# Masks and divisions of two chunks moved to TensorE, and a third chunk's attention started earlier

## The chip, the cores and the metric

The kernel runs on one core of one Trainium2 chip. The metric is the device time of one execution in microseconds; lower is better. The engines are PE (TensorE matmuls; PEld is its weight loads), DVE (VectorE), ACT (ScalarE), POOL (GpSimd) and SP (SyncE, whose queue issues all loads and stores here).

## The reference

Attention with 4 batches, 8 heads, 768 positions and 64 elements per head, and behind it a gated feed-forward layer over its 3,072 tokens. Cut to what matters:

```python
k_sum = k.reshape(B, H, 24, 32, D).max(axis=3)       # a key per block of 32
v_sum = v.reshape(B, H, 24, 32, D).mean(axis=3)
scores_l = scale * q @ k.T, masked to |i - j| < 16    # scale = 1/8
scores_s = scale * q @ k_sum.T + log(32)
a = softmax(concat([scores_l, scores_s]))             # sum + 1e-9 in the division
x = (a @ concat([v, v_sum])) as (3072, 512)
out = ((x @ w_a) * (x @ w_b)) @ w_out                 # d_ff = 1536
```

## The kernel before

**Tokens.** The 3,072 tokens are 12 chunks of 256 (`u` = 0 to 11, three per batch), a chunk is two groups of 128. A group's attention needs the window's 96 keys (and 24 block keys) of each of two halves. Its scores for four pairs of heads fill two PSUM banks of 128x512.

**A group's attention** in chunks 0 and 1: PE transposes the queries (`turn`, L401), ACT copies them (`qT`), PE makes the scores (L600), DVE scales them and adds the mask on the way to SBUF (L619) and takes the maxima (L627), ACT makes eight exponentials with their sums (L636), DVE the reciprocals (L643, L649), POOL divides the 128x512 halves (L653), PE transposes them (L401), ACT copies (L669), PE multiplies by the values (L698), and ACT and DVE split the result into a high and a low part, `x` (L706, L709). Chunks from 2 on use no PE for transposes: DVE does them in 32x256 steps, twelve per group (L685 for the probabilities, L863 for the queries). Chunk 0 has two sets of buffers for its two groups, chunk 1 one set (`s`, `pt`, `vw`, `qT`, banks `o2` and `o3`).

**Weights.** `w_a`, `w_b` and `w_out` come in as 36 parts of 512 KB; `convert(j)`, j = 0 to 17, splits two parts at a time into high and low halves: ACT writes the shifted high bits to SBUF and to bank `c0` (L294), DVE makes three passes per half (L309, L327 into `c1`, L333), ACT casts the high half (L369), POOL makes the low half in two passes (L374, L380). The parts stand in the order a0, b0, out0, a1, and so on.

**Feed-forward.** `item(n, u, f)` is one of 12 slices `f` of `d_ff` of chunk `u`: 24 matmuls up (L906), ACT copy, DVE product (L926), ACT cast (L928), DVE remainder (L931), and 6 matmuls down (L942) into `o0`/`o1` (chunk 1: `o2`/`o3`). An up needs the chunk's `x` and the a and b parts of its slice, a down the out part. `x` has two buffers (`u % 2`). The items of chunks 0 and 1 alternate, chunk 0 ahead by LAG = 4 slices; from chunk 2 on the items stand chunk by chunk.

**Order.** Every step is handed to `Work` with an engine, a rank, an estimate of its length and the names of what it reads and writes. `emit` is a list scheduler: it picks, by rank and by estimated readiness, which step stands next on which engine. So the order on each engine is fixed when the program is built, and an engine waits in order at run time. Ranks (L229): CHAIN 0, FIRST 1 (chunk 0), CONVERT 2 + j/4, NEXT 3 (chunk 1), SOON 5 (chunk 2), PREP 5.5, LATER 6. The attention of chunk 2 and of chunk 3 is handed in behind item (1, 11), and its scores use banks `c0` and `c1`, which the conversions use too. Its second group's probabilities lie in `S1`, a conversion buffer; `qin`, its queries' buffer, serves the last conversions as slot "Q".

Of the kernel before, what the change touches and what calls it, by code (L numbers as in the profile page):

```python
# [15 lines left out]
ALU = mybir.AluOpType  # L16
# [68 lines left out]
def attention_moe(  # L85
# [27 lines left out]
    SIGNS = 2  # L113
    FILL = 2
# [114 lines left out]
    CHAIN, FIRST, CONVERT, NEXT, SOON, PREP, LATER = 0, 1, 2, 3, 5, 5.5, 6  # L229
# [38 lines left out]
    spaces["Q"] = qin.rearrange("p c x -> p (c x)")  # L268
    slots = [("S0", 0), ("S0", 2), ("S1", 2), ("Q", 0), ("S0", 0), ("S0", 2), ("S1", 2), ("S0", 0)]

    def convert(j):
# [3 lines left out]
        if j < NW - 4:  # L275
            space = {12: "W16", 13: "W17"}.get(j, ("W17", "W16", "W15", "S0")[j % 4])
            places = [(space, 0, 2), (space, 1, 3)]
            single = j < 2
        else:
            places = [slots[2 * (j - NW + 4) + h] for h in range(2)]  # L280
            places = [(n, x, x + 1) for n, x in places]
            single = True
# [161 lines left out]
    def first_keys():  # L444
        n = P // BLK
        for i in range(S // P):
# [6 lines left out]
            bk = f"o{i % 4}"  # L453
# [134 lines left out]
    def scores(u, t, qT, qk, s, sk, banks, lead=None):  # L588
        kind = 0 if t == 0 else 2 if t == S // P - 1 else 1
        rank = rank_of(u)  # L590
        m, mk = nml[t % 2], f"nml{t % 2}"

        def fn():
            for c in range(NP):
                for h in range(2):
                    hs = slice(h * D, (h + 1) * D)
                    for e in range(2):
# [5 lines left out]
                            start=True, stop=True, tile_position=(h * D, e * QT),  # L603
                        )

        if lead is None:
            pe(-1, 1.2, [qk] + KT, banks, fn)
        else:
# [22 lines left out]
        for h in range(2):
            l = m[:, 1, h, :]
            for c in range(NP):
                act(
                    rank, 0.385, [f"{mk}m{h}", sk[h]], [f"{mk}l{h}{c}"],
                    lambda h=h, c=c: nc.scalar.activation(  # L636
                        s[h][:, c, :], s[h][:, c, :], AF.Exp, bias=m[:, 0, h, c : c + 1],
                        scale=1.0, accum_out=m[:, 1, h, c : c + 1],
                    ),
                )  # L640
            dve(
                rank, 0.1, (), [f"{mk}l{h}{c}" for c in range(NP)],
                lambda l=l: nc.vector.tensor_scalar(  # L643
                    out=l, in0=l, scalar1=1e-9, scalar2=None, op0=ALU.add
# [3 lines left out]
                rank, 0.1, (), [f"{mk}l{h}{c}" for c in range(NP)],  # L648
                lambda l=l: nc.vector.reciprocal(out=l, in_=l),  # L649
            )  # L650
            pool(
                rank, 1.05, [f"{mk}l{h}{c}" for c in range(NP)], [sk[h]],
                lambda h=h, l=l: nc.gpsimd.tensor_tensor(  # L653
                    out=s[h], in0=s[h], in1=l[:, :, None].broadcast_to([P, NP, P]),
                    op=ALU.mult,
                ),
            )

    def transposes(u, t, s, sk, banks):
# [360 lines left out]
```

## Time and profile before

| | |
|---|---|
| time, median of 3 runs | 712.74 us (712.11 to 713.24) |
| time of the profiled execution | 712.94 us |
| its span on the chip | 711.2 us |
| PE busy | 680.2 us (96% of the span) |
| DVE, ACT, POOL busy | 438.8, 271.9, 190.1 us |
| matmuls up (L906), down (L942) | 420.7 us; 158.0 + 90.7 us |

The span is what the trace covers; 1.7 us of the time lie outside of it. "busy" is the time an engine's instructions took, "idle before" what the engine waited before a group, with the instruction that released it. A line number is one of the listing above.

### The profile page before, as it was taken

How to read it: one execution, taken by the hardware profiler on the slowest of the kernel's cores; microseconds unless marked ns; L12 is line 12 of the kernel's file. 1: busy time of each engine (PE TensorE's matmuls, PEld its weight loads, DVE VectorE, ACT ScalarE, POOL GpSimd, SP SyncE). 2: the span in 40 equal slices, each digit the busy share in tenths (PEclk: the TensorE clock that was granted, in tenths of full speed). 3: DMA queues.
4: the chain of work that ended last, by engine and by line, in shares of the span. 5: the costliest groups of instructions: out<-in, count | busy, mean ns of one | idle time of the engine just before them, and what ended most of it. 6: DMA issues, size and time to landing. Idle time of an engine off the chain costs nothing.

```text
span 711.2 us, 15046 instructions
## 1 busy us (share of the span) xinstructions
PE 680.2 (96%) x5952; PEld 625.5 (88%) x5952; DVE 438.8 (62%) x992; ACT 271.9 (38%) x815; POOL 190.1 (27%) x228
## 2 busy tenths in 40 slices
PE   6676799999999999999999999999999999999997
PEld 5475699998989999999999999999999999999996
DVE  3989898598727677766765776673673662321221
ACT  3878886442333332333332423432332331211211
POOL 5589899412334244113010101110110110000000
PEclk9979999999999999999999999999999999999999
DMA  9996353347214334522210330310310100000000
GB/s 230 283 332 201 127 150 126 63 87 162 54 53 117 80 76 94 95 46 60 71 35 2 82 68 1 86 24 1 83 24 1 53 22 1 31 1 1 30 1 29
DMA packets 154942, 54.83 MB, mean 77 GB/s; under 512 B 132456, under 2 KB 147816, under 8 KB 154872
## 3 DMA queue, kind: packets, MB, share of 16 engines
q1 hardware_dynamic: 154872, 53.88, 31.1%
q8 instruction: 46, 0.75, 0.4%
q14 instruction: 24, 0.20, 0.1%
HBM read 47.12 MB, written 6.29 MB: 75 GB/s over the span
## 4 chain that ended last, share of the span: by engine, by line
PE 82%; DVE 6%; SPq 4%; DMA 3%; ACT 2%; POOL 2%; issue 1%; DVEq 0%; POOLq 0%; ACTq 0%
PE h L906 50%; PE o L942 25%; SPq L225 2%; SPq L254 2%; PE o L698 2%; PE o L600 2%; PE c L600 2%; PE c L698 1%; POOL S L540 1%; DVE pt L685 1%; DMA raw<-in_moe_w_a_dram 1%; DMA S<-in_v_dram 1%; DVE ksum L470 1%; DMA space<-in_k_dram 0%; ACT s L636 0%
## 5 line engine op out<-in xcount | busy, mean ns | idle before, releaser
L906 PEld LDWEIGHTS h<-x,w 128*128 128x128 f32 x3456 | 418.0, 190 | 15.2 <-DVE x L709 2.7
L906 PE MATMUL h<-x,w 128*128 128x256 f32 x3456 | 420.7, 279 | 4.1 <-DVE x L709 2.6
L926 DVE TENSOR_TENSOR h<-h,g 128x256 f32<-128x256 f32 x144 | 62.1, 431 | 173.0 <-ACT g L923 171.6
L942 PE MATMUL o<-w,gh 128*128 128x512 f32 x576 | 158.0, 397 | 4.9 <-ACT gh L928 4.9
L923 ACT COPY g<-h 128x256 f32<-128x256 f32 x144 | 53.7, 373 | 283.7 <-PE h L906 283.0
L942 PEld LDWEIGHTS o<-w,gh 128*128 128x128 f32 x576 | 98.9, 188 | 23.1 <-ACT gh L928 6.6
L653 POOL TENSOR_TENSOR s<-s,nml 128x512 f32<-128x512 f32 x44 | 45.8, 1042 | 257.7 <-DVE nml L649 253.9
L685 DVE STREAM_TRANSPOSE pt<-s 32x256 f32<-32x256 f32 x228 | 99.4, 436 | 8.8 <-POOL s L653 3.9
L942 PE MATMUL o<-w,gl 128*128 128x512 f32 x288 | 90.7, 397 | 0.0
L636 ACT ACTIVATE s<-s,nml 128x128 f32<-128x128 f32 x176 | 68.6, 393 | 50.5 <-DVE nml L627 50.3
L931 DVE TENSOR_TENSOR gl<-h,gh 128x256 fp32r<-128x256 f32 x144 | 60.5, 420 | 30.4 <-ACT gh L928 29.3
L928 ACT CAST gh<-h 128x256 fp32r<-128x256 f32 x144 | 53.5, 372 | 63.7 <-DVE h L926 61.7
L942 PEld LDWEIGHTS o<-w,gl 128*128 128x128 f32 x288 | 53.8, 189 | 11.9 <-issue 0.5
L540 POOL TENSOR_TENSOR S<-S 96x512 f32<-96x512 f32 (+3 forms) x48 | 33.6, 699 | 55.2 <-DMA S<-in_v_dram 44.9
L636 ACT ACTIVATION_READ_ACCUMULATOR s<-s,nml 128x1 f32 x176 | 33.3, 189 | 0.0
L643 DVE TENSOR_SCALAR nml<-nml 128x4 f32<-128x4 f32 x48 | 11.9, 249 | 29.6 <-ACT s L636 29.4
L627 DVE TENSOR_REDUCE nml<-s 128x4 f32<-128x512 f32 x44 | 27.8, 667 | 0.0
L374 POOL TENSOR_TENSOR space<-space,w 128x1024 f32<-128x1024 f32 (+1 forms) x13 | 26.8, 2062 | 3.5 <-ACT w L369 2.7
L380 POOL TENSOR_TENSOR w<-space 128x1024 fp32r<-128x1024 f32 (+1 forms) x13 | 26.7, 2054 | 0.9
L294 ACT ACTIVATE S<-raw 128x1024 f16<-128x1024 f32 (+1 forms) x20 | 23.0, 1149 | 4.8 <-DVE space L309 1.8
L294 ACT ACTIVATE c<-raw 128x512 f32<-128x512 f32 x36 | 23.2, 644 | 1.9 <-DVE space L309 1.2
L436 POOL COPY kT<-ksum 128x144 f32<-128x144 f32 x16 | 4.8, 309 | 57.9 <-DVE ksum L518 44.5
(99 smaller groups left out, 460.4 us busy)
## 6 DMA issues: line engine op xcount, KB each, us to landing
raw<-in_moe_w_a_dram SPq DMA_DIRECT2D x12, 512.0 KB
raw<-in_moe_w_b_dram SPq DMA_DIRECT2D x12, 512.0 KB
raw<-in_moe_w_out_dram SPq DMA_DIRECT2D x12, 512.0 KB
out_dram<-S SPq DMA_DIRECT2D x24, 256.0 KB
qin<-in_q_dram SPq DMA_DIRECT2D x160, 32.0 KB
S<-in_v_dram SPq DMA_DIRECT2D x24, 192.0 KB
vw<-in_v_dram SPq DMA_DIRECT2D x19, 192.0 KB
vw<-in_v_dram SPq DMA_DIRECT2D x19, 128.0 KB
```

Source lines behind the costliest of these rows:

```text
L294: nc.scalar.mul(out=zhalf[:, lo:hi] if out is None else out, in_=high.bitcast(F32), mul=2.0**-112)
L540: lambda: nc.gpsimd.tensor_tensor(out=out, in0=i0, in1=i1, op=ALU.add),
L600: nc.tensor.matmul(bank[banks[h]][es, c * P : (c + 1) * P], qT[hs, c, es], kT[hs, c, c0 : c0 + P], start=True, stop=True, tile_position=(h ...
L636: lambda h=h, c=c: nc.scalar.activation(s[h][:, c, :], s[h][:, c, :], AF.Exp, bias=m[:, 0, h, c : c + 1], scale=1.0, accum_out=m[:, 1, h, ...
L653: lambda h=h, l=l: nc.gpsimd.tensor_tensor(out=s[h], in0=s[h], in1=l[:, :, None].broadcast_to([P, NP, P]), op=ALU.mult,),
L685: lambda js=js, qs=qs: nc.vector.transpose(out=pv[js, :, qs], in_=sv[qs, :, js]),
L906: nc.tensor.matmul(ps, w[:, c, part, :], x[xpart][:, c, :], start=(i == 0), stop=(i == n - 1))
L923: act(CHAIN, 0.38, [hk], [gk], lambda: nc.scalar.copy(out=g, in_=pa))
L926: lambda: nc.vector.tensor_tensor(out=pa, in0=pb, in1=g, op=ALU.mult),
L928: act(CHAIN, 0.41, [hk], [ghk], lambda: nc.scalar.copy(out=gh, in_=pa))
L931: lambda: nc.vector.tensor_tensor(out=gl, in0=pa, in1=gh.bitcast(F32), op=ALU.subtract),
L942: nc.tensor.matmul(bank[ok[j]], (gh if first else gl)[:, js], w[:, :, part, :], start=(f == 0 and first and part == 0), stop=(f == NF - 1 ...
```

## The change

- **Masks.** For chunks 0 and 1, PE writes the mask into the score banks as a product of mask and identity (L598 of the changed kernel), and the scores accumulate on it (L610). The factor 1/8 goes into the copy of the queries (L833). DVE takes the maxima straight from PSUM (L643), the exponentials read PSUM and leave their sums there (L655). L619's eight DVE instructions for these groups are gone.
- **Divisions.** DVE multiplies the identity by the reciprocals (L677), and the PE product of probabilities and that diagonal (L698) divides and transposes at once. The eight POOL multiplies and the eight plain transposes are gone.
- **Two sets** of `s`, `pt`, `vw`, `qT` and of banks (`o0`/`o1`, `o2`/`o3`) serve groups 2 and 3 (chunk 1) as well; `begin` and `end` in `first_attention` hand all four groups in. NEXT goes from 3 to 2.3, LAG from 4 to 2. The key transposes use `c0`, `c1`, `o2`, `o3`.
- **Third chunk.** `attention` becomes a generator; chunk 2's is advanced behind conversion 7 (query loads), 9 (first group to its transposes), 17 (second group's scores) and behind item (0, 11) (the rest). `qin` is no conversion slot any more, and chunk 2's second group uses `s` instead of `S1`.
- Chunks from 2 on keep their masks on DVE, divisions on POOL (now L685), transposes on DVE (now L725).

The diff, cut to its core:

```diff
+    AHEAD = (7, 9, 17)
...
-    CHAIN, FIRST, CONVERT, NEXT, SOON, PREP, LATER = 0, 1, 2, 3, 5, 5.5, 6
+    CHAIN, FIRST, CONVERT, NEXT, SOON, PREP, LATER = 0, 1, 2, 2.3, 5, 5.5, 6
...
-    spaces["Q"] = qin.rearrange("p c x -> p (c x)")
-    slots = [("S0", 0), ("S0", 2), ("S1", 2), ("Q", 0), ("S0", 0), ("S0", 2), ("S1", 2), ("S0", 0)]
+    slots = [("S0", 0), ("S0", 2), ("S1", 2)]
...
-            bk = f"o{i % 4}"
+            bk = ("c0", "c1", "o2", "o3")[i % 4]
...
+        masked = u < FILL
+
+        def masks():
+            for h in range(2):
+                nc.tensor.matmul(
+                    bank[banks[h]].rearrange("p (c x) -> p c x", x=P), ident,
+                    mask[:, kind, None, :].broadcast_to([P, NP, P]), start=True, stop=False,
+                )
 
...
-                            start=True, stop=True, tile_position=(h * D, e * QT),
+                            start=not masked, stop=not masked or c == NP - 1,
+                            tile_position=(h * D, e * QT),
...
+        if masked:
+            pe(rank + 0.1, 1.8, [], banks, masks)
...
+        x = [bank[n].rearrange("p (c x) -> p c x", x=P) for n in banks] if masked else s
+        xk = banks if masked else sk
...
+            sums = x[h][:, :, 0] if masked else l
...
+            if masked:
+                d, dk = diag
+                dve(
+                    rank, 0.6, lk + [xk[h]], dk[h],
+                    lambda h=h, r=r, d=d: nc.vector.tensor_tensor(
+                        out=d[:, h], in0=ident[:, None, :].broadcast_to([P, NP, P]),
+                        in1=r[:, :, None].broadcast_to([P, NP, P]), op=ALU.mult,
+                    ),
+                )
+            else:
+                pool(
+                    rank, 1.05, lk, [sk[h]],
+                    lambda h=h, r=r: nc.gpsimd.tensor_tensor(
+                        out=s[h], in0=s[h], in1=r[:, :, None].broadcast_to([P, NP, P]),
+                        op=ALU.mult,
+                    ),
+                )
...
+            def turned(h):
+                for c in range(NP):
+                    nc.tensor.matmul(
+                        bank[banks[h]][:, c * P : (c + 1) * P], s[h][:, c, :], d[:, h, c, :],
+                        start=True, stop=True,
+                    )
...
+        pts = [PD, (x.rearrange("p (h c x) -> p h c x", h=2, x=P), [[key[0]], [key[1]]])]
+        def begin(g, bk):
+            u, i = g // G, g % G
+            x, key = queries[g]
+            rank = rank_of(u) + 0.2 * i
+            pe(rank, 0.85, [key], [bk], lambda: turn(bank[bk], x))
             act(
-                FIRST, 0.6, [f"h{t}"], [qTk[t]],
-                lambda t=t: nc.scalar.copy(
-                    out=qT[t], in_=bank[f"h{t}"].rearrange("p (c x) -> p c x", x=P)
+                rank, 0.6, [bk], [qTk[i]],
+                lambda: nc.scalar.mul(
+                    out=qT[i], in_=bank[bk].rearrange("p (c x) -> p c x", x=P), mul=0.125
                 ),
             )
+            scores(u, g, qT[i], qTk[i], s[i], sk[i], [f"o{2 * i}", f"o{2 * i + 1}"], pts[i])
+
+        def end(g, bk):
+            u, i = g // G, g % G
+            transposes(u, g, s[i], sk[i], [f"o{2 * i}", f"o{2 * i + 1}"], pts[i])
...
+        end(0, "h1")
+        load_values(0, 2, vbuf, VK[:3], 20.5)
+        begin(2, "o0")
+        end(1, "h0")
+        load_values(0, 3, vw1, vk1[:3], 20.7)
+        begin(3, "o2")
+        end(2, "o0")
+        end(3, "o2")
...
         if u == FILL:
+            yield
+            begin(0)
+            turned(0)
+            yield
+            begin(1)
+            yield
+            values(*end(0))
+            bring(1)
+            turned(1)
+            values(*end(1))
+        elif u == FILL + 1:
...
-    LAG = 4
+    LAG = 2
...
+    third = attention(FILL)
...
+        if j in AHEAD:
+            next(third)
         item(n, u, f)
-        if (u, f) == (1, NF - 1):
-            attention(2)
-            attention(3)
-        elif f == NF - 1 and 1 < u < NU - 2:
-            attention(u + 2)
+        if (u, f) == (0, NF - 1):
+            next(third)
+        elif f == NF - 1 and u < NU - 2:
```

**PE at the start of the program.** `space8`/`space9` hold keys, `o0` to `o3`, `c0`, `c1`, `h0`, `h1` are PSUM banks. Before:

```order
L401 MATMUL o0_71<-ident_66,space8_188 128x128 x4
L401 MATMUL o1_72<-ident_66,space8_188 128x128 x4
L401 MATMUL o2_73<-ident_66,space8_188 128x128 x4
L401 MATMUL o3_74<-ident_66,space8_188 128x128 x4
L401 MATMUL o0_71<-ident_66,space9_189 128x128 x4
L401 MATMUL o1_72<-ident_66,space9_189 128x128 x4
L401 MATMUL h0_75<-ident_66,space9_189 128x128 x4
L401 MATMUL h1_76<-ident_66,space9_189 128x128 x4
L600 MATMUL o0_71<-kT_79,qT_183 64x128 x2
L600 MATMUL o1_72<-kT_79,qT_183 64x128 x2
```

After:

```order
L598 MATMUL o0_71<-mask_86,ident_66 128x512
L598 MATMUL o1_72<-mask_86,ident_66 128x512
L401 MATMUL c0_77<-ident_66,space8_188 128x128 x4
L401 MATMUL c1_78<-ident_66,space8_188 128x128 x4
L401 MATMUL o2_73<-ident_66,space8_188 128x128 x4
L401 MATMUL o3_74<-ident_66,space8_188 128x128 x4
L401 MATMUL c0_77<-ident_66,space9_189 128x128 x4
L401 MATMUL c1_78<-ident_66,space9_189 128x128 x4
L598 MATMUL o2_73<-mask_86,ident_66 128x512
L598 MATMUL o3_74<-mask_86,ident_66 128x512
L401 MATMUL h0_75<-ident_66,space9_189 128x128 x4
L401 MATMUL h1_76<-ident_66,space9_189 128x128 x4
```

The first two mask products now stand ahead of the key transposes, the other two ahead of the queries' transposes; the scores (L610) follow behind them.

**ACT between the first and the third conversion.** L294 and L369 are conversion steps, L655 an exponential of chunk 1, L833, L710, L747 and L706 copies of attention, L976 an item's copy. Before:

```order
L706 CAST x0_0_169<-h0_75 128x4x128
L369 CAST w1_471<-space16_194 128x4x128
L294 ACTIVATE c0_77<-raw2_275 128x512
L369 CAST w1_471<-space16_194 128x4x128
L294 ACTIVATE S1_187<-raw3_281 128x1024
L294 ACTIVATE c0_77<-raw3_281 128x512
L923 COPY g0_173<-h0_75 128x256
L369 CAST w2_519<-space15_193 128x8x128
L294 ACTIVATE c0_77<-raw3_281 128x512
```

After:

```order
L833 ACTIVATE qT_183<-o0_71 128x512
L833 ACTIVATE space12_192<-o2_73 128x512
...
L655 ACTIVATE s_163,o0_71<-o0_71,nml0_184 128x128 x2
L294 ACTIVATE c0_77<-raw2_280 128x512
L655 ACTIVATE s_163,o0_71<-o0_71,nml0_184 128x128 x2
L655 ACTIVATE s_163,o1_72<-o1_72,nml0_184 128x128 x2
L294 ACTIVATE S1_187<-raw3_289 128x1024
...
L976 COPY g0_173<-h0_75 128x256
L655 ACTIVATE s_163,o1_72<-o1_72,nml0_184 128x128 x2
L981 CAST gh0_175<-h0_75 128x256
L710 COPY pt_164<-o0_71 128x512
L655 ACTIVATE space11_191,o2_73<-o2_73,nml1_185 128x128 x4
L369 CAST w2_615<-space15_193 128x8x128
```

Ahead of conversion 2's high half (`w2`), ACT now has twelve exponentials of chunk 1 and three of its copies (two L833, one L710); before, it had none of them.

**POOL at the last conversion.** `s_163` is the buffer of chunk 2's probabilities, `S0`/`S1` are conversion buffers. Before:

```order
L374 TENSOR_TENSOR S1_187<-S1_187,w17_1414 128x512
L380 TENSOR_TENSOR w17_1414<-S1_187 128x4x128
L374 TENSOR_TENSOR S0_186<-S0_186,w17_1414 128x512
L380 TENSOR_TENSOR w17_1414<-S0_186 128x4x128
L653 TENSOR_TENSOR s_163<-s_163,nml0_184 128x512 x2
L653 TENSOR_TENSOR S1_187<-S1_187,nml1_185 128x512 x2
```

After:

```order
L374 TENSOR_TENSOR S0_186<-S0_186,w17_1628 128x512
L540 TENSOR_TENSOR S1_187<-S1_187 96x512
L540 TENSOR_TENSOR S1_187<-S1_187 96x256
L540 TENSOR_TENSOR S1_187<-S1_187 96x128
L380 TENSOR_TENSOR w17_1628<-S0_186 128x4x128
L685 TENSOR_TENSOR s_163<-s_163,nml1_185 128x512
L374 TENSOR_TENSOR S0_186<-S0_186,w17_1628 128x512
L685 TENSOR_TENSOR s_163<-s_163,nml1_185 128x512
L380 TENSOR_TENSOR w17_1628<-S0_186 128x4x128
```

The division of chunk 2's second group (L685) now stands in between the steps of conversion 17, and so does work on values in `S1` (L540); before, both groups' divisions (L653) came behind that conversion.

**PE around the same place.** `w13` to `w17` are converted weights; L610 are the scores of chunk 2's second group, L739 its first group's values.

```order
L995 MATMUL o2_73<-w13_1328,gh0_175 128x512 x2
L995 MATMUL o3_74<-w13_1328,gh0_175 128x512 x2
L995 MATMUL o2_73<-w13_1328,gl0_177 128x512
L995 MATMUL o3_74<-w13_1328,gl0_177 128x512
L610 MATMUL c0_77<-kT_79,qT_183 64x128 x2
L610 MATMUL c1_78<-kT_79,qT_183 64x128 x2
...
L610 MATMUL c1_78<-kT_79,qT_183 64x128 x2
L995 MATMUL o0_71<-w16_1570,gh1_176 128x512 x2
L995 MATMUL o1_72<-w16_1570,gh1_176 128x512 x2
L739 MATMUL c0_77<-pt_164,vw0_165 64x64 x2
```

The scores of the second group stand in front of the downs with `w16` and the first group's values right behind; 20 ups and 19 downs of chunks 0 and 1 are ahead of them. Before, both groups' scores stood further up, behind 17 ups and 15 downs, and behind 18 ups.

## Rows read from the trace of the kernel before

**Rows 1.** Busy by stretch: start:end, length, PE, PEld, DVE, ACT, POOL, clock, DMA share, GB/s
```profile
35.91:85.19 49.28, 36.16 (x303) 31.01 (x303) 43.30 (x77) 40.42 (x83) 41.71 (x22) 0.88 0.72 230
85.19:143.00 57.81, 57.81 (x474) 54.04 (x472) 46.22 (x88) 39.20 (x84) 45.95 (x28) 1.00 0.44 111
143.00:170.00 27.00, 26.69 (x235) 24.34 (x234) 26.07 (x72) 9.01 (x30) 5.86 (x8) 1.00 0.56 113
85.19:711.23 626.04, 621.01 (x5453) 577.27 (x5450) 371.65 (x873) 208.39 (x669) 127.56 (x139) 1.00 0.24 55
```

**Rows 2.** The same view, line L906 alone, from the start to 85.19 us
```profile
0.00:85.19 85.19, 19.15 (x121) 18.57 (x121) 0.92 0.89 241
```

**Rows 3.** Chain that ended last, 96 to 101 us: start, us, engine, line
```profile
96.95 2.74 PE h L906 x24
99.69 1.37 PE o L942 x6
```

**Rows 4.** Waits of PE behind 90 us: total, times, longest us
```profile
PE c L698 <- DMA vw<-S: 0.5, 1, 0.5
PE o L942 <- ACT gh L928: 0.3, 1, 0.3
```

**Rows 5.** Timeline of PE: start, us, line, out<-in, form, count [idle before <-releaser]
```profile
11.35 1.11 PE L401 MATMUL h<-ident,space 128*128 128x128 f32 x4
14.47 1.98 PE L600 MATMUL o<-kT,qT 64*64 64x128 f32 x32 [0.47 <-POOL kT L436]
24.38 0.66 PE L401 MATMUL o<-ident,s 128*128 128x128 f32 x4 [0.77 <-POOL s L653]
24.88 1.03 PE L788 MATMUL h<-space,space 128*128 128x256 f32 x4
35.91 5.49 PE L906 MATMUL h<-x,w 128*128 128x256 f32 x24 [2.61 <-DVE x L709]
132.57 1.10 PE L600 MATMUL c<-kT,qT 64*64 64x128 f32 x32
138.85 1.10 PE L600 MATMUL c<-kT,qT 64*64 64x128 f32 x32
165.13 1.15 PE L698 MATMUL c<-pt,vw 128*64 128x64 f32 x32
169.46 2.75 PE L906 MATMUL h<-x,w 128*128 128x256 f32 x22
```

**Rows 6.** PE by stretch: start:end, length, busy (count), granted clock, DMA
```profile
68.60:72.00 3.40, 3.40 (x18) 0.51 1.02 345
```

**Rows 7.** Timeline of ACT, DVE and POOL, single instructions
```profile
18.48 0.40 ACT L636 ACTIVATE s<-s,nml 128x128 f32<-128x128 f32 x1 [3.12 <-DVE nml L627]
43.47 0.59 ACT L856 COPY qT<-o 128x512 f32<-128x512 f32 x1
58.34 0.64 ACT L294 ACTIVATE c<-raw 128x512 f32<-128x512 f32 x1
60.02 0.68 DVE L327 TENSOR_SCALAR c<-space 128x512 int32<-128x512 int32 x1
42.83 2.39 POOL L374 TENSOR_TENSOR space<-space,w 128x1024 f32<-128x1024 f32 x1 [1.99 <-ACT w L369]
85.66 2.43 POOL L374 TENSOR_TENSOR space<-space,w 128x1024 f32<-128x1024 f32 x1
90.55 2.41 POOL L374 TENSOR_TENSOR space<-space,w 128x1024 f32<-128x1024 f32 x1
```

**Rows 8.** Timeline of SP: the loads of the third chunk's queries
```profile
120.67 7.73 SPq L225 DMA_DIRECT2D qin<-in_q_dram  x16
```

**Rows 9.** Costliest groups of the page: busy us, mean ns | idle, releaser
```profile
L926 DVE TENSOR_TENSOR h<-h,g 128x256 f32<-128x256 f32 x144 | 62.1, 431 | 173.0 <-ACT g L923 171.6
L653 POOL TENSOR_TENSOR s<-s,nml 128x512 f32<-128x512 f32 x44 | 45.8, 1042 | 257.7 <-DVE nml L649 253.9
L685 DVE STREAM_TRANSPOSE pt<-s 32x256 f32<-32x256 f32 x228 | 99.4, 436 | 8.8 <-POOL s L653 3.9
```

More of the change, by code (lines that the diff above doesn't have):

```diff
@@ L279, in convert @@
         else:
-            places = [slots[2 * (j - NW + 4) + h] for h in range(2)]
+            places = [slots[(2 * (j - NW + 4) + h) % 3] for h in range(2)]
             places = [(n, x, x + 1) for n, x in places]
@@ L647, in scores @@
             dve(
-                rank, 0.1, (), [f"{mk}l{h}{c}" for c in range(NP)],
-                lambda l=l: nc.vector.reciprocal(out=l, in_=l),
-            )
[L651 to L659, printed above, removed]
+                rank, 0.15, [xk[h]] if masked else [], lk,
@@ L660, in transposes @@
+    def transposes(u, t, s, sk, banks, diag=None):
         rank = rank_of(u)
         if u < FILL:
+            d, dk = diag
+            def turned(h):
[3 more added lines that the diff above has]
+                        start=True, stop=True,
+                    )
             for h in range(2):
                 pe(
-                    -1, 0.85, [sk[h]] + [f"{sk[h]}{c}" for c in range(NP)], [banks[h]],
@@ L724, in attention_moe @@
     PT = [f"pt{i}{j}" for i in range(4) for j in range(4)]
+    PD = (pbuf, [[x for x in PT if (x[2] in "01") == (h == 0)] for h in range(2)])
     def first_attention():
@@ L807, in first_attention @@
             )
-        transposes(0, 0, s0, SK, ["o0", "o1"])
-        values(0, 0, vbuf, VK, "h1")
-        transposes(0, 1, s1, sk[1], ["o2", "o3"])
-        values(0, 1, vw1, vk1, "h0")
-        x, qk = spot(6)
-        rows = x.rearrange("p (i x) -> p i x", i=2)
-        for i in range(G):
-            load(
-                21, 262.0, 215, (), [qk[i]], rows[:, i, :].rearrange("p (h d) -> p h d", d=D),
-                heads(q[0, :, CH + i * P : CH + (i + 1) * P, :]),
-            )
-        return rows, qk
+        end(0, "h1")
[6 more added lines that the diff above has]
+        end(3, "o2")
     lead = []
@@ L835, in attention @@
         t0 = G * r
-        if u < FILL:
-            rows, qk = second
-        else:
-            qk = []
-            work.add("-", 0, 0, 0, (), ["Q.0", "Q.1"], lambda: None)
-            for c in range(NP):
-                qk += blocks(98, f"qin.{c}", qin[:, c, :], q, b, c, r * CH, ["Q.0", "Q.1"])
+        qk = []
+        for c in range(NP):
+            qk += blocks(98, f"qin.{c}", qin[:, c, :], q, b, c, r * CH)
         def bring(i):
@@ L867, in end, with begin, turned @@
-        def end(i, s, sk):
-            transposes(u, t0 + i, s, sk, banks[i])
-            values(u, t0 + i, vbuf, VK, vbank[i])
+        def begin(i):
+            dve(
+                rank, 0.62, qk, ["qT"],
+                lambda: nc.vector.transpose(out=qTs, in_=qin[:, :, i * P : (i + 1) * P]),
+            )
+            scores(
+                u, t0 + i, qTs, "qT", s0, SK, banks[i], lead=lead.pop() if lead else None
+            )
+        def turned(i):
+            transposes(u, t0 + i, s0, SK, banks[i])
```

124 lines of the change are left out of this document (57 added, 67 removed).

## Prediction

> **What bounds the kernel now.** I read the busy times by stretch first. From 85.19 us on PE is busy 621.01 of 626.04 us [rows 1]: whatever comes later, the time is the matmuls that are left at that point, so only what happens before can gain or lose. From 35.91 to 85.19 PE is busy 36.16 of 49.28 us, while DVE has 43.30, POOL 41.71 and ACT 40.42: weights are being converted, and chunk 1's attention lies in between. What did PE get done? Its up products up to 85.19 are 121 records in 19.15 us [rows 2], five ups of 24 (and the first of a sixth), where five at full speed take 13.7, since an up takes 2.74 and a down 1.37 [rows 3]. So five items of 4.12, 20.6 us of work, in the 49 us behind the first product at 35.91 [rows 5]. A change earns its keep if PE has done more by the time at which it saturates, and does not lose that later. Behind 90 us PE waits for little: 0.5 us for a value load and 0.3 us for one ACT cast [rows 4].
>
> The sum is made against the profiled execution, 712.94 us (span 711.2, 1.7 outside), 0.2 above the median 712.74.
>
> **The start: worse.** Two mask products stand ahead of the key transposes. No row shows one of 512 columns; the nearest is a product of twice 256 fp32 columns, 1.03 us [rows 5]. At the start PE is slower: the same four transposes take 1.11 us at 11.35 and 0.66 at 24.38, the 32 score products 1.98 at 14.47 and 1.10 at 132.57 [rows 5]. So a pair costs between 2.1 us and, at half speed, 4.1. I take 3.9, since it stands first of all; the second pair falls where PE waits for keys and ACT. On the other side DVE no longer adds masks: two passes of 0.68 [rows 7] ahead of the first exponentials are gone. The exponentials, at 18.48 before [rows 7], come 2.7 later (3.9, less 1.4, and 0.2 for the accumulating scores); the ends are +1 and +4.5. POOL's four divisions of chunk 0 at 1.042 [rows 9] become four DVE products at 0.68 [rows 7], 1.4 less in a row, of which I count 1.1; the diagonal products take 1.03 a half by the same 512-column row in place of 0.66, beside other work. First up: 35.91 + 2.7 - 1.1 = **37.5**.
>
> **Conversions 0 to 8: later, then even.** ACT now carries chunk 1's attention between the conversions: ahead of conversion 2's cast stand twelve exponentials of 0.40 and three copies of 0.59 [rows 7], 6.6 us. With the 1.6 from the start, and 0.8 taken off because ACT waits there at times before, POOL starts conversion 2 at 50.2 instead of 42.83 [rows 7], and ends it near 55. The last four exponentials and three copies push conversion 5 to about 71.9. From there POOL needs 4.89 us per conversion (85.66 to 90.55 [rows 7]), with no divisions between: the eight of chunks 0 and 1 took 1.042 each [rows 9]. Conversion 8 ends at 71.9 + 14.7 = 86.6 and 9 at 91.5, about one us behind before (its second POOL pass follows the start at 85.66, and the next conversion starts at 90.55). So weights are not earlier. What is earlier is chunk 1's `x`: about 67 us by the same walk; before, its two groups went one behind the other through one set of buffers.
>
> **PE up to 89.3: ahead.** In its order PE waits for conversion 2 (to 55) and for the last diagonal product (to about 61.5); from 71 it has work without gaps, because chunk 1's items can use weights that lie ready. Done at 71: four ups and three downs. From there to 89.3 I walk the order: conversions 5, 6 and 7 are there when their turn comes, and four more ups, three downs, 1.1 us of the third chunk's first scores (32 products, 1.10 [rows 5]) fit, with 1.7 us lost to one stretch at half clock such as 68.60 to 72.00 (0.51 granted [rows 6]). That makes 8 x 2.75 + 6 x 1.37 = 30.2, and 1.1 of scores. Before, it was 20.6 + (89.3 - 85.19) = 24.7. **Lead: 6.6 us.** LAG 2 is part of this and costs nothing by itself.
>
> **89 to 143: some of it back.** DVE becomes the limit. From 91.8, when by my walk conversion 9's passes are through, it has eight conversions of six passes of 0.69 (33.1), the first group's twelve transposes at 0.436 [rows 9] (5.2) with maxima, reciprocals and the next queries' transpose (2.7), and eleven items with two steps of 0.43 [rows 9] (9.4): 50.4, so to 142.2 without a gap, to 144.0 at the 26.07 of 27.00 that DVE reaches between 143 and 170 [rows 1]. The second group's scores need `c0` and `c1`, which conversion 17 uses to the end: 142.7, say. PE gets there, 20 ups and 19 downs, at 89.3 + 81.1 - 30.2 = 140.2. It **loses 2.5**. The query loads, 7.73 us of SP's queue at 120.67 [rows 8], now stand early, ahead of parts of conversion 4; by my walk those parts are not needed before ACT reaches them, so they cost nothing (if they are late, see the last rival).
>
> **143 to the third chunk.** From the second group's scores (142.7) to its `x` lie mask, maxima, eight exponentials of 0.40, POOL's two divisions of 1.042 [rows 9] among conversion 17's steps, twelve transposes of 0.436, 1.15 of value products [rows 5] and the split: about 20.7 us. PE has the scores, the other group's values and 17.8 us of items, 20.3, to do meanwhile: it **loses 0.4**. The first product of chunk 2, at 169.46 before [rows 5], comes at about 165.5. Later chunks are unchanged; the waits of 0.5 and 0.3 [rows 4] should go, as loads stand earlier and the order is new: 0.8.
>
> **Sum:** 712.9 - 6.6 + 2.5 + 0.4 - 0.8 = **708.4 us**. The ends of the start (+1 and +4.5 for +2.7) and of the DVE stretch (142.2 to 144.0) give this case 705.5 to 711.2.
>
> **Rivals.**
> 1. *The masks hurry the clock.* PE starts at half speed, by the transposes at 11.35 against 24.38 [rows 5], and is then busy only in pieces. The mask products let it work through from the start, so it may be granted the higher level sooner; then the pair costs 2.1, and what follows is shorter too: 1.8 us less, **706.6**. Against it: PE has been working in pieces for ten us before, and 14.47 is slow still. In the Trainium skill, "TensorE: Matmul & The Clock Gate", Part 1 (The HAM clock gate) says that the array starts at half rate and is released by recent activity; by that rule the first pair would run at half rate and the transposes behind it sooner at the full one, and the sum would come to 706.6 or less, against 708.4 by the row at 14.47, which is still slow; that the array starts slow, this trace agrees (1.11 against 0.66).
> 2. *DVE keeps pace.* If ACT's conversions of the last weights run as now and PE is not held at `c0`, the 2.5 and the 0.4 are not lost: **705.5**. For it: between 85.19 and 143 DVE is busy 46.22 of 57.81 us [rows 1]; against it, the sum of its work.
> 3. *Slower: the third chunk's second group comes too late.* Its scores stand behind conversion 17 on `c0`, its division among that conversion's POOL steps. From its scores at 138.85 to its values at 165.13 [rows 5] it took 26.3 us before, with DVE full. If it takes as long from 144, the values come at 170.3, and PE has run out of items by then: 712.9 + 5.2 - 0.8 = **717.3**. It decides from values later than 165.9. For it: DVE 26.07 of 27.00 [rows 1], and preparation of the next batch competes; against it: in the before half of those 26 us were other transposes, and the first group's are now done earlier.
> 4. *The query loads delay the weights.* If the 7.73 us [rows 8] ahead of the fifth conversion's parts push it by 4 us, the lead is 2.6: **712.4**, the same.
>
> **Chances.** What a measurement of this kernel can tell is about 0.2%, 1.4 us. Forecast 0.46, rivals 0.15 (1), 0.13 (2), 0.16 (3), 0.10 (4). Faster 0.46 + 0.15 + 0.13 = 0.74, same 0.10, slower 0.16. The range holds the forecast's own, rivals 1, 2 and 4, and the milder half of rival 3; its low end is rivals 1 and 2 together (703.7): 703.5 to 716.5.
>
> **What would show it.** Mask pair at the start: 3.9 us; first exponential at 21.2; first up at 37.5; conversion 2's POOL start at 50.2; chunk 1's second `x` at 67; PE saturated from 71 with eight ups by 89.3; the second group's scores at 142.7 behind a PE wait of about 2.5 for a DVE pass into `c1`; first product of chunk 2 at 165.5. I am wrong if first ups come later than 40, if conversion 8 ends behind 90, or if PE waits before 170 for an `x` of chunk 2 for more than two us.

## The result and the profile after

The changed kernel takes 705.45 us (median of 4 runs, 703.89 to 707.55), against 712.74: a ratio of 0.990 (95% interval 0.9866 to 0.9934). The forecast was 708.4 in a range of 703.5 to 716.5. The profiled execution took 703.89 us, its span is 702.2; to the profiled one before it is 9.05 us less, to be explained below.

The page's first part, busy time and share of the span:

```profile
PE 682.5 (97%) x6000; PEld 626.5 (89%) x6000; DVE 439.8 (63%) x992; ACT 271.2 (39%) x815; POOL 182.3 (26%) x220
```

PE's total busy time hardly moved (680.2 before), though it now has the masks and diagonals to do as well: the gain is idle time that is gone, and less slow work. The ups alone take 416.3 us instead of 420.7; before, the first of them ran at half the clock (5.49 us at 35.91 [rows 5]), and so did the stretch of [rows 6]. How much of these 4.4 us reached the end is not shown, as PE waited behind both places. By stretch, in the columns of [rows 1]:

```profile
35.91:85.19 49.28, 44.98 (x408) 39.84 (x411) 45.53 (x84) 43.10 (x88) 40.28 (x20) 0.93 0.93 270
85.19:143.00 57.81, 55.94 (x464) 51.10 (x457) 54.12 (x100) 39.05 (x84) 45.01 (x29) 1.00 0.36 86
143.00:170.00 27.00, 26.62 (x225) 25.05 (x224) 23.17 (x65) 9.04 (x30) 11.13 (x17) 1.00 0.68 143
85.19:702.20 617.01, 610.48 (x5368) 566.98 (x5360) 372.94 (x869) 206.76 (x665) 127.28 (x139) 1.00 0.23 52
```

Between 35.91 and 85.19 PE is busy 44.98 us, 8.8 more than before; POOL has less to do, DVE more. From 85.19 on 617.0 us are left instead of 626.0. DVE is busy 54.12 of 57.81 us in the next stretch, where it had 46.22 [rows 1].

PE's timeline at the start, in the columns of [rows 5]:

```profile
4.45 3.78 PE L598 MATMUL o<-mask,ident 128*128 128x512 f32 x4 [4.45 <-POOL mask L173]
...
10.68 0.66 PE L401 MATMUL c<-ident,space 128*128 128x128 f32 x4
...
18.29 1.10 PE L610 MATMUL o<-kT,qT 64*64 64x128 f32 x32 [1.40 <-POOL kT L436]
...
37.29 1.98 PE L598 MATMUL o<-mask,ident 128*128 128x512 f32 x4
39.20 1.10 PE L610 MATMUL o<-kT,space 64*64 64x128 f32 x32
40.24 3.10 PE L959 MATMUL h<-x,w 128*128 128x256 f32 x24
```

The mask pair costs 3.78 us. The transposes behind it then run at 0.66 per four where [rows 5] has 1.11 at the same time, and the scores at 1.10 instead of 1.98. Two pairs of masks and the scores of chunk 1 (the last of them at 37.29 and 39.20) stand ahead of the first up at 40.24. Behind it:

```profile
46.45 1.50 PE L698 MATMUL o<-pt,s 128*128 128x128 f32 x8 [2.22 <-DVE pt L677]
...
58.90 1.13 PE L698 MATMUL o<-space,space 128*128 128x128 f32 x8 [1.36 <-DVE space L677]
...
62.54 5.62 PE L959 MATMUL h<-x,w 128*128 128x256 f32 x48
...
84.79 1.10 PE L610 MATMUL c<-kT,qT 64*64 64x128 f32 x32
```

PE waits for DVE's diagonals, 2.22, 0.72 and 1.36 us, and from 58.90 on for nothing until the first row below, which lies in the stretch where DVE is full; the others are the end of chunk 1:

```profile
111.95 1.20 PE L995 MATMUL o<-w,gh 128*128 128x512 f32 x4 [1.16 <-ACT gh L981]
...
139.26 1.10 PE L610 MATMUL c<-kT,qT 64*64 64x128 f32 x32
...
157.30 1.15 PE L739 MATMUL c<-pt,vw 128*64 128x64 f32 x32 [0.38 <-DVE x L750]
...
161.26 4.94 PE L959 MATMUL h<-x,w 128*128 128x256 f32 x42
```

The first product of chunk 2 begins at 161.26, where it was 169.46 [rows 5]. ACT's first exponential, and POOL's passes (the first of conversion 2, the last of 5 and of 8):

```profile
20.76 0.37 ACT L655 ACTIVATE s<-o,nml 128x128 f32<-128x128 f32 x1
...
48.24 2.38 POOL L374 TENSOR_TENSOR space<-space,w 128x1024 f32<-128x1024 f32 x1 [4.50 <-ACT w L369]
...
66.52 2.42 POOL L380 TENSOR_TENSOR w<-space 128x1024 fp32r<-128x1024 f32 x1
...
82.88 2.40 POOL L380 TENSOR_TENSOR w<-space 128x1024 fp32r<-128x1024 f32 x1
```

### The profile page after: what moved, and what is told of

Read it like the earlier page. It is cut to its first block, busy times and chain, and to the rows that moved or that the text cites. A ratio compares the mean times of both kernels' runs of the same rounds, so it can differ in the third digit from the quotient of the medians.

```text
span 702.2 us, 15117 instructions
## 1 busy us (share of the span) xinstructions
PE 682.5 (97%) x6000; PEld 626.5 (89%) x6000; DVE 439.8 (63%) x992; ACT 271.2 (39%) x815; POOL 182.3 (26%) x220
## 4 chain that ended last, share of the span: by engine, by line
PE 85%; DVE 7%; ACT 4%; DMA 2%; issue 1%; POOL 0%; SPq 0%; POOLq 0%; DVEq 0%; ACTq 0%
PE h L959 51%; PE o L995 27%; PE c L739 2%; PE c L610 2%; PE o L739 2%; DVE pt L725 1%; DMA raw<-in_moe_w_b_dram 1%; PE o L610 1%; ACT s L655 1%; DVE c L327 1%; ACT c L294 1%; ACT S L294 1%; DVE ksum L470 1%; PE o L598 1%; DVE gl L984 0%
## 5 line engine op out<-in xcount | busy, mean ns | idle before, releaser
L959 PE MATMUL h<-x,w 128*128 128x256 f32 x3456 | 416.3, 277 | 0.0
L976 ACT COPY g<-h 128x256 f32<-128x256 f32 x144 | 53.7, 373 | 277.6 <-PE h L959 276.8
L725 DVE STREAM_TRANSPOSE pt<-s 32x256 f32<-32x256 f32 x240 | 104.7, 436 | 8.3 <-POOL s L685 4.0
L685 POOL TENSOR_TENSOR s<-s,nml 128x512 f32<-128x512 f32 x40 | 41.7, 1042 | 243.1 <-DVE nml L670 241.5
L655 ACT ACTIVATE s<-s,nml 128x128 f32<-128x128 f32 x160 | 62.5, 393 | 49.5 <-DVE nml L643 46.8
L540 POOL TENSOR_TENSOR S<-S 96x512 f32<-96x512 f32 (+3 forms) x48 | 33.5, 698 | 49.6 <-DMA S<-in_v_dram 39.8
L655 ACT ACTIVATION_READ_ACCUMULATOR s<-s,nml 128x1 f32 x160 | 30.3, 190 | 0.0
L380 POOL TENSOR_TENSOR w<-space 128x1024 fp32r<-128x1024 f32 (+1 forms) x13 | 26.8, 2064 | 1.0
L294 ACT ACTIVATE S<-raw 128x1024 f16<-128x1024 f32 (+1 forms) x20 | 23.1, 1153 | 6.5 <-DVE S L309 4.6
L643 DVE TENSOR_REDUCE nml<-s 128x4 f32<-128x512 f32 x40 | 25.2, 667 | 0.0
L294 ACT ACTIVATE c<-raw 128x512 f32<-128x512 f32 x36 | 23.2, 645 | 4.0 <-DVE space L320 1.5
```

Of the source, the lines that this page charges most:

```text
L294: nc.scalar.mul(out=zhalf[:, lo:hi] if out is None else out, in_=high.bitcast(F32), mul=2.0**-112)
L540: lambda: nc.gpsimd.tensor_tensor(out=out, in0=i0, in1=i1, op=ALU.add),
L655: lambda h=h, c=c, sums=sums: nc.scalar.activation(s[h][:, c, :], x[h][:, c, :], AF.Exp, bias=m[:, 0, h, c : c + 1], scale=1.0, accum_out= ...
L685: lambda h=h, r=r: nc.gpsimd.tensor_tensor(out=s[h], in0=s[h], in1=r[:, :, None].broadcast_to([P, NP, P]), op=ALU.mult,),
L725: lambda js=js, qs=qs: nc.vector.transpose(out=pv[js, :, qs], in_=sv[qs, :, js]),
L959: nc.tensor.matmul(ps, w[:, c, part, :], x[xpart][:, c, :], start=(i == 0), stop=(i == n - 1))
```

## Experiments

Theory: chunk 1's two groups go through attention side by side and some 20 us earlier, which gives PE work from weights that lie ready, and it saturates at about 60 us instead of 85. Rivals: the masks and divisions as such (relief of DVE, or of POOL), the clock, the loads' order, LAG. The table has every kernel; "values" is the start of the value products of chunk 1's second group on PE (83.64 us before), "PE busy" and clock are of 35.91 to 85.19 us. "Lead" is what PE has done by 89.3 us, counted as in the forecast (2.75 per up, 1.37 per down, 1.1 for chunk 2's first scores), less the 24.7 of before; "lost" is the part of it that does not arrive in the span (711.2 before). Both come from one profile of each kernel.

| kernel | median, us | ratio to before (95%) | values | PE busy, clock | lead, lost |
|---|---|---|---|---|---|
| changed kernel | 705.45 | 0.990 (0.9866 to 0.9934) | 60.89 | 44.98, 0.93 | 10.0, 1.0 |
| its repeat | 706.29 | 0.9906 (0.9888 to 0.9923) | 63.00 | 41.43, 0.97 | 8.0, 1.3 |
| no advance of chunk 2 | 714.52 | 1.0024 (1.0013 to 1.0035) | 63.59 | 43.25, 0.90 | 6.7, 10.3 |
| NEXT 3 | 722.77 | 1.0124 (1.0107 to 1.0142) | 73.56 | 38.06, 0.86 | 1.9, 9.6 |
| old masks and divisions | 711.57 | 0.9981 (0.9968 to 0.9994) | 60.85 | 36.92, 0.83 | 6.3, 4.7 |
| old masks only | 707.93 | 0.995 (0.993 to 0.9969) | 59.34 | 40.06, 0.86 | 7.1, 1.6 |
| diagonals on POOL | 711.11 | 0.999 (0.9973 to 1.0007) | 65.84 | 39.58, 0.90 | 4.9, 4.2 |
| masks behind key transposes | 707.68 | 0.9933 (0.9919 to 0.9947) | 64.32 | 42.48, 0.93 | 7.3, 0.6 |
| one set for chunk 1 | 719.54 | 1.0108 (1.0092 to 1.0123) | 75.06 | 32.91, 0.83 | -5.9, 1.4 |
| LAG 4 | 710.08 | 0.9971 (0.9957 to 0.9984) | 62.28 | 41.77, 1.00 | 8.2, 4.6 |
| late query loads | 704.10 | 0.989 (0.9877 to 0.9904) | 60.61 | 45.14, 0.93 | 9.9, 1.0 |
| late query loads, NEXT 2.0 | 706.00 | 0.9919 (0.9902 to 0.9935) | 58.12 | 44.00, 0.97 | 9.6, 2.7 |
| late query loads, LAG 1 | 706.67 | 0.9923 (0.9909 to 0.9937) | 61.33 | 42.92, 0.97 | 9.0, 2.8 |

The order on every engine comes out of one list scheduler, so each edit moves more than its own instructions; the prices below are of the edit with what the scheduler made of it. Early values alone do not decide: "old masks only" has them earlier than the changed kernel (59.34) and is slower. And in five kernels (no advance, NEXT 3, old masks and divisions, diagonals on POOL, LAG 4) 4 to 10 us of the lead go behind 89.3 us, so that the waits up to 85 us, which are shown for some of them, are only part of their price.

**The changed kernel again.** No edit.

> The changed kernel once more, for a second profile. Its four times lay at 703.9 to 704.0 and at 706.9 to 707.6. If the clock alone separates them, a profile near 707 shows the same orders and about 3.4 us more of half clock at a place where PE has no idle time, and the stages from 90 us on are as before.

706.29 us (703.91 to 708.32, 6 runs), profiled 706.23. In this profile the expectation's reason, the clock alone, is not what differs: the mean clock is no lower (0.997 against 0.995). It is lower, 0.989 to 0.993, in those four of the two kernels' ten runs that took over 706.5 us; of them there is no trace, so their cause stays open. In the profiled repeat SP's queue shows what varies. In the changed kernel's first profile the third chunk's query loads stand here:

```profile
29.99 12.61 SPq L226 DMA_DIRECT2D qin<-in_q_dram  x16
...
43.67 1.68 SPq L226 DMA_DIRECT2D vw<-in_v_dram  x3
...
48.79 0.62 SPq L255 DMA_DIRECT2D raw<-in_moe_w_b_dram  x1
49.45 0.50 SPq L255 DMA_DIRECT2D raw<-in_moe_w_out_dram  x1
```

Sixteen loads hold the queue for 12.61 us, and behind them stand the values and, at 48.79 and 49.45, the two parts of conversion 5, which the trace of before shows at 37.50 and 38.94. In the repeat the sixteen hold it for 13.25 us, the two parts come at 49.32 and 49.98, and ACT has to wait for both, 0.5 and 0.7 us:

```profile
54.62 0.64 ACT L294 ACTIVATE c<-raw 128x512 f32<-128x512 f32 x1 [0.49 <-DMA raw<-in_moe_w_b_dram]
55.91 1.37 ACT L294 ACTIVATE S<-raw 128x1024 f16<-128x1024 f32 x1 [0.66 <-DMA raw<-in_moe_w_out_dram]
```

That moves DVE's last diagonal of chunk 1 by 0.7 us (58.06 to 58.74). PE stands 3.10 us ahead of its product instead of 1.36,

```profile
59.58 2.05 PE L698 MATMUL o<-space,space 128*128 128x128 f32 x8 [3.10 <-DVE space L677]
```

and what follows runs at a low clock. From 58.5 to 62.5 us, first in the repeat, then in the first profile (columns of [rows 6]):

```profile
58.50:62.50 4.00, 2.92 (x11) 0.59 1.13 281
```

```profile
58.50:62.50 4.00, 3.60 (x46) 1.00 0.90 259
```

Two waits of half a us become 2.0 on PE: the third chunk's first scores stand at 86.82 instead of 84.79.

**Late query loads.** The loads wait for conversion 4.

```diff
+        late = ["done4"]
-            qk += blocks(98, f"qin.{c}", qin[:, c, :], q, b, c, r * CH)
+            qk += blocks(98, f"qin.{c}", qin[:, c, :], q, b, c, r * CH, late if u == FILL else ())
```

> The third chunk's query loads wait for conversion 4 to be done, so the 12.6 us that they hold SP's queue from 30 to 42.6 us fall behind 60 us; value loads and the weights of conversions 3 to 5 come earlier. Theory (loads do not bound this stretch, DVE and ACT do): 705 to 707.5, the waits of PE for value loads (1.4 us in the repeat of the changed kernel) gone. Rival (the prediction's fourth: the loads delay the weights): conversion 3 and the following start 2 to 4 us earlier, 702 to 704.

704.10 us, all four runs within 704.01 to 704.69: between the two ranges, just above the rival's. The values are issued at 31.65 and the first twelve of the query loads at 54.80:

```profile
31.65 4.21 SPq L226 DMA_DIRECT2D vw<-in_v_dram  x3
...
54.80 9.25 SPq L226 DMA_DIRECT2D qin<-in_q_dram  x12
```

The span is that of the changed kernel's first profile (702.3 against 702.2). Conversions 3 and 5 start at 53.08 and 63.76 instead of 53.29 and 64.03, not the 2 to 4 us earlier of the rival. So the loads do not bound that course, as the theory said, but they are what other runs lose by: in the profiled repeat 2 us, and the changed kernel's spread of 4 us is gone with the loads moved, here and in the two kernels below that have them late too (1.1 and 0.8 us, with clocks of 0.994 to 0.998 in all their runs). The prediction's fourth rival is real, in a small form, in part of the runs. This version has the lowest ratio of all against the before of its own runs, though within the interval of the changed kernel's, and its slowest run is below the changed kernel's median.

**No advance of the third chunk.**

```diff
-    AHEAD = (7, 9, 17)
+    AHEAD = ()
...
-            next(third)
+            for _ in third:
+                pass
```

> The third chunk's attention is not advanced between conversions but handed in as a whole behind item (0, 11); the rest is as in the changed kernel. Theory (early attention of chunk 1 fills PE from 60 us on, and the advance lets the lead survive): the lead at 89 us stays 9 to 10 us, but PE runs out of items at about 157 and waits for chunk 2's x until 165 to 169: 708 to 712 us. Rival (the lead alone is the gain, chunk 2 was ready in time anyway): 704 to 707.

714.52 us, more than either expected. PE's busy time before 85 us lies between those of the changed kernel's two profiles (43.25); the lead at 89.3 is 6.7 us, not the 9 to 10 expected, in a profile that is the slowest of twelve runs (716.47). Then PE runs out of items before chunk 2's second `x` is there (most of its values are made at 166.34, in the changed kernel at 157.30); PE's waits behind 143 us:

```profile
PE c L739 <- DVE pt L725: 2.5, 1, 2.5
PE h L959 <- ACT x L747: 0.7, 1, 0.7
```

and what follows, again, at a granted clock of 0.69:

```profile
168.40:176.90 8.50, 8.36 (x52) 0.69 0.68 155
```

So the idle time is paid a second time: the first product of chunk 2 comes at 168.35, only 1.1 us earlier than before, and from there to the end it takes 4.7 us longer than before, 2.6 of them by this clock. The lead is worth nothing without the advance.

**Rank NEXT.**

```diff
-    CHAIN, FIRST, CONVERT, NEXT, SOON, PREP, LATER = 0, 1, 2, 2.3, 5, 5.5, 6
+    CHAIN, FIRST, CONVERT, NEXT, SOON, PREP, LATER = 0, 1, 2, 3, 5, 5.5, 6
```

> Rank NEXT back at 3, so chunk 1's attention stands behind the conversions 0 to 3 in rank. Theory (early attention of chunk 1): its second x comes later, PE saturates some us later than 60, part of the gain is lost: 706 to 710. Rival (what counts is that masks and divisions left DVE and POOL): no change, 704 to 707.

722.77 us: the theory's direction, at four times its size, and slower than before. The lead shrinks to 1.9 us, and 9.6 are lost behind 89.3. With chunk 1 behind the conversions in rank, PE's two longest waits up to 85 us are for DVE (an item's remainder) and for conversions:

```profile
PE h L959 <- DVE gl L984: 4.2, 1, 4.2
PE h L959 <- POOL w L380: 3.5, 2, 3.1
```

**One set for chunk 1.** In `begin` and `end`, groups 2 and 3 take set 0, and group 3 begins behind the end of group 2.

```diff
-            u, i = g // G, g % G
+            u, i = g // G, 0 if g >= G else g
```

> Chunk 1's two groups go one behind the other through one set of s, pt, vw, qT and banks; chunk 0 keeps two sets, all else as in the changed kernel. Theory (early attention needs two sets): the second x comes 10 to 15 us later than 64, PE has gaps until about 75, 710 to 715. Rival (the rank alone does it): 705 to 708.

719.54 us, more than the 710 to 715 expected: at 89.3 PE is 5.9 us behind the kernel before. PE's waits from 33 to 85 us are the chain of one group at a time:

```profile
PE o L698 <- DVE pt L677: 6.6, 2, 6.4
PE o L401 <- DVE x L750: 3.9, 1, 3.9
PE o L698 <- ACT s L655: 3.9, 1, 3.9
```

**Old masks and divisions.** DVE adds the masks, POOL divides, PE transposes; sets, ranks and the advance stay.

```diff
-        masked = u < FILL
+        masked = False
...
-                    lambda h=h: turned(h),
+                    lambda h=h: turn(bank[banks[h]], s[h].rearrange("p c x -> p (c x)")),
```

> Masks of chunks 0 and 1 back on DVE, their divisions on POOL, plain transposes on PE; two sets of buffers, the order rules and the advance stay. Theory (early attention by two sets of buffers and order): most of the gain stays, 704 to 708, with the first scores about 4 us earlier as no mask products stand ahead. Rival (relief of DVE and POOL is the gain): most of it goes, 710 to 713.

711.57 us: the rival's number. But its reason, relief of engines that are full, is not what the waits show (33 to 85 us):

```profile
PE o L401 <- POOL s L685: 4.8, 2, 3.2
PE o L739 <- DMA vw<-in_v_dram: 4.4, 2, 3.8
```

The division stands in POOL's queue among conversion passes of up to 2.4 us, and value loads come late, which is no matter of masks or divisions. The next two kernels take back one part each.

**Diagonals on POOL.** The row sums stay in SBUF, POOL builds the diagonals.

```diff
-            sums = x[h][:, :, 0] if masked else l
+            sums = l
...
-                dve(
-                    rank, 0.6, lk + [xk[h]], dk[h],
-                    lambda h=h, r=r, d=d: nc.vector.tensor_tensor(
+                pool(
+                    rank, 1.05, lk, dk[h],
+                    lambda h=h, r=r, d=d: nc.gpsimd.tensor_tensor(
```

> Only the diagonals go from DVE to POOL (eight of about 1.04 us in place of 0.69 on DVE); masks and diagonal products stay on PE. Theory (POOL's queue is the loss): chunk 1's x comes later by two to four us, 708 to 711. Rival (DVE is the limit until 74 us): DVE has 5.5 us less to do, 702 to 705.

711.11 us, just above the theory's range: DVE lost eight steps of 0.69 us and nothing was gained. PE's waits from 33 to 85 us:

```profile
PE o L698 <- POOL pt L677: 5.3, 2, 2.7
PE h L959 <- DVE gl L984: 2.5, 1, 2.5
```

POOL's queue is only one half of this. Each of chunk 1's four diagonals starts 0.17 us behind its reciprocal, and POOL stood idle for 0.41 to 0.61 us before it. The reciprocal is late because DVE's step ahead of it, which adds 1e-9 to the sums, ends with POOL's conversion pass:

```profile
55.91 2.35 POOL L380 TENSOR_TENSOR w<-S 128x1024 fp32r<-128x1024 f32 x1
55.97 2.32 DVE L664 TENSOR_SCALAR nml<-nml 128x4 f32<-128x4 f32 x1
58.87 1.04 POOL L677 TENSOR_TENSOR space<-ident,nml 128x512 f32<-128x512 f32 x1 [0.61 <-DVE nml L670]
```

The four steps take 0.21, 1.14, 0.24 and 2.32 us, and each ends 0.02 to 0.03 us behind a pass of POOL. In the changed kernel, where the sums lie in PSUM, the same step takes 0.16 us in the middle of a pass (POOL's L380 from 55.78 to 58.18):

```profile
57.65 0.16 DVE L664 TENSOR_SCALAR o<-o 128x4 f32<-128x4 f32 x1
```

So the chain meets POOL's passes twice, in POOL's queue and in DVE's step. This edit moves the diagonals and the sums together, as does "old masks and divisions" (0.36 to 1.23 us for the step, and each division 0.14 to 0.15 us behind its reciprocal); which of the two counts for how much is not shown.

**Old masks only.** An add on DVE, in place in the score bank.

```diff
-        if masked:
-            pe(rank + 0.1, 1.8, [], banks, masks)
...
+                        out=x[h], in0=x[h], in1=mask[:, kind, None, :].broadcast_to([P, NP, P]),
+                        op=ALU.add,
```

> Only the masks of chunks 0 and 1 go back to DVE (an add in place in the score bank, eight of about 0.69 us); the divisions stay PE products. Theory (the way through POOL's queue is what olddiv lost by, masks are worth little): 703 to 707, since the start gains the mask pair's 3.8 us and DVE pays 8 x 0.69 = 5.5 us. Rival (DVE is the limit from 19 to 74 us, and the masks' relief of it is the gain): 709 to 712.

707.93 us, just outside the theory's range and short of the rival's. The masks on PE are worth about 2 us by the medians and 3 by the ratios (0.995 against the repeat's 0.9906). "Old masks and divisions" lost 2 to 4 us more than this kernel, so which of the two parts is the larger is not shown.

**Masks behind the key transposes.** The first pair waits for the fifth key tile.

```diff
-            pe(rank + 0.1, 1.8, [], banks, masks)
+            pe(rank + 0.1, 1.8, [spot(2)[1][0]] if u == 0 else [], banks, masks)
```

> The first pair of mask products stands behind the fifth key transpose instead of ahead of the first, the second pair behind the queries' transposes; nothing else changes. Theory (the pair of 3.78 us is on the chain to the first exponentials): keys and scores come 2 to 4 us earlier, first up at 37 to 38.5, and 702 to 705. Rival (the masks hurry the clock): the transposes then run at 1.1 us instead of 0.66, and nothing is gained, 705 to 708.

707.68 us, no gain, and both mechanisms are seen:

```profile
4.22 2.18 PE L401 MATMUL c<-ident,space 128*128 128x128 f32 x8 [4.22 <-DMA space<-in_k_dram]
...
9.46 1.08 PE L401 MATMUL c<-ident,space 128*128 128x128 f32 x4 [0.18 <-DMA space<-in_k_dram]
...
12.28 0.60 PE L401 MATMUL c<-ident,space 128*128 128x128 f32 x4
...
37.04 3.01 PE L959 MATMUL h<-x,w 128*128 128x256 f32 x24
39.88 1.88 PE L598 MATMUL o<-mask,ident 128*128 128x512 f32 x4
```

Eight transposes now take 2.18 us, four 1.08, until 12.28; with the masks ahead they ran at 0.66 from 10.68 on at the latest. Scores and first up came 3 us earlier, as the theory said. But the scheduler now put the masks of chunk 1's second group behind the first up (39.88), and its values came at 64.32 instead of 60.89. What an earlier start is worth by itself is therefore not shown; with this order it brought nothing.

**LAG 4.**

```diff
-    LAG = 2
+    LAG = 4
```

> LAG back at 4, nothing else. Theory (PE has work without gaps from 60 us on because chunk 1's items can use the first weights as soon as its x is there; with LAG 4 chunk 0's next slices stand ahead and wait for weights that are still being converted): PE waits for POOL's conversions again between 55 and 85 us, 708 to 712. Rival (the prediction's sentence that LAG costs and brings nothing by itself): 705 to 707.

710.08 us, as the theory said, though the waits for conversions are only part: PE's waits behind 33 us add up to about 12 us instead of 7.3, 3.4 of them for ACT's casts of items, 1.0 for POOL.

**Further along the same ways.** With the late loads, NEXT at 2.0 and LAG at 1.

> The late query loads, and rank NEXT at 2.0 instead of 2.3, so that chunk 1's attention stands ahead of conversion 1 and all later ones. Theory (2.3 already puts chunk 1 as early as DVE allows; what moves ahead of it is paid by later weights): no gain over the late loads alone, 704 to 708. Rival (each step of rank still brings some): 700 to 703.

> The late query loads, and LAG 1. Theory (LAG 2 gives PE work from the weights that lie ready; with LAG 1 chunk 1 would need its x a slice earlier and chunk 0 loses one slice of distance): PE waits for chunk 1's x at about 57 us, 704 to 708. Rival (the trend from 4 to 2 goes on): 701 to 703.5.

706.00 (0.9919, 0.9902 to 0.9935) and 706.67 us (0.9923, 0.9909 to 0.9937): both behind the late loads alone and inside the theory's ranges: neither way brings more, and 2.3 and 2 are the best of the values tried.

## Why the prediction was right, and where its sum was off

The sign, the range and the mechanism held: lead before 89 us, partly given back. The sum was 3 us too cautious against the median and 4.5 against the profiled execution. One of the forecast's own signs of being wrong came true (the first up later than 40), and one term came out near its size for another reason than the one given (89 to 143), which is luck. By its steps:

- **The start.** Mask pair 3.78 (3.9 forecast), first exponential 20.76 (21.2). The first up failed: 40.24 instead of 37.5, beyond the bound that I had named. I worked out when its `x` and weights are ready, and conversion 0's last pass did end at 37.6; I did not see that 6 us of masks and scores of chunk 1 stand ahead on PE. No cost of it shows: "masks behind key transposes" had the first up at 37.04 and was no faster.
- **Conversions.** Conversion 2 started at 48.24 (50.2 forecast), 5 ended at 68.94 (71.9), 8 at 85.28 (86.6): later, then even, as forecast, and 1 to 3 us earlier than that. Before, the pass behind conversion 8 started at 85.66 [rows 7]. So the weights are not what made the gain.
- **PE up to 89.3: the term that was mis-sized.** By 89.3 it had done 8.2 ups and 8 downs, 33.6 us, and 1.1 of scores: a lead of 10.0 over the 24.7 before, where I had 6.6. Of the 3.4, some 1.4 lie ahead of 71 (4.5 ups instead of 4, as PE's last wait ends at 58.90 and not at 61.5, and DVE's half of chunk 1's second `x` starts at 63.20 where I had that `x` at 67), the rest behind it: I put the stretch at half clock there (1.7), while it came from 50 on, where PE's wait that ends at 58.90 hid it (columns of [rows 6]):

```profile
50.00:54.00 4.00, 4.00 (x43) 0.52 1.09 307
```

- **89 to 143: near in size, not in place.** 1.9 us were lost instead of 2.5: 1.16 and 0.71 behind ACT's casts of items, and none at `c0`, where the second group's scores stood at 139.26 without a wait (142.7 forecast). The first is ACT's own queue, which the forecast did not have: from 104.70 to 115.5 ACT works without a wait, and the copy of the item at 109.15 stands behind its other steps, 2.5 us behind the end of the up. Ahead of the second, ACT had waited for a full DVE:

```profile
109.15 0.36 ACT L976 COPY g<-h 128x256 f32<-128x256 f32 x1
...
125.69 0.80 ACT L294 ACTIVATE S<-raw 128x512 f16<-128x512 f32 x1 [2.65 <-DVE S L309]
```

- **143 to chunk 2.** 0.38 lost (0.4); the 0.8 saved later came (span from chunk 2's first product: 541.7 before, 540.9 after).
- With the measured terms the sum is 712.9 - 10.0 + 1.9 + 0.4 - 0.8 = 704.4, half a us from the profiled 703.89.
- **Slips in the forecast's sums.** The two ends named for the start and the DVE stretch give 706.2 to 711.5, not 705.5 to 711.2, and PE's work behind the second group's scores (1.10, 1.15 and 17.8) adds up to 20.1, not 20.3. Neither decides anything.
- **Rivals.** The first (clock) happens in its first part: the transposes behind the masks run at full speed earlier. In the Trainium skill, "TensorE: Matmul & The Clock Gate", Part 1 (The HAM clock gate), says the array starts at half rate and is released by activity; the two starts agree with it (0.66 at 10.68, against 1.08 at 9.46 with the masks later). But no run shows that it is worth time. The second did not happen: 1.9 us were lost, with DVE busy 54.12 of 57.81 us. The third did not happen either (values at 157.30), but "no advance", with values at 166.34, shows that it is what the change avoids. The fourth happens in part of the runs.
- Which parts made the gain: none alone. Without the second set, the rank or the advance the kernel is slower than before; with the divisions or their diagonals on POOL it is within 0.2% of before. That the divisions count through waits for POOL's passes, in POOL's queue and in DVE's step on the sums, and not through work, was not in the forecast.

## What to carry to other kernels

A chain of short steps that meets another engine's long ones is best taken out of their way, even onto an engine that is busier: here the diagonals on DVE at 0.69 us, with their sums in PSUM, beat POOL's 1.04 by several us of waiting, though DVE was the fuller one. Look for the meeting place on both engines, in the queue and in steps that take longer than their like. An early lead is worth what the next stage lets through, so look for the next resource (here chunk 2's `x`) before the first stall is removed. When a kernel's times spread over half a per cent, compare two profiles at the first instruction that differs: here a set of small loads that stood 25 us earlier than they had to.

## What was not expected of the hardware

- **Waits and the clock.** In two places a wait of PE in a full stretch cost up to twice its length: 2.46 us for transposes in "no advance" were followed by 8.5 us at a granted clock of 0.69, some 2.6 us more, and 1.7 us of added wait in the repeat by 4 us at 0.59. It is no rule: the wait for chunk 1's second diagonal product, 2.22 us at 46.45, was followed by 0.52 in the changed kernel, but waits of 2.30 us for the same product, at 45.98 in the repeat and 45.99 in LAG 4, by a granted 1.00 in every 4 us up to 56. What decides is not shown.
- **A short step of DVE can last as long as a pass of POOL.** The add on 128x4 sums took 0.16 us in PSUM and up to 2.32 us in SBUF, where it ended with the pass ("diagonals on POOL").
- **Where an exponential leaves its sum sets its pace.** Reading PSUM with the sums in PSUM, as in the changed kernel, one follows the other by 0.46 us, though each takes 0.37; with the sums in SBUF ("diagonals on POOL") by 0.34, and before, reading and writing SBUF, by 0.39. So the sums in PSUM cost ACT 0.12 us each.
- **Small loads and the queue.** The sixteen query loads held SP's queue for 12.61 us where the DMA engines moved 200 GB/s, against 7.73 [rows 8] at 59 GB/s.
